# A gated spectral and MLP block with its gradients: the gate as row sums on VectorE, the first products by pairs of token blocks, the last tile in halves

## The chip, the core and the metric

The kernel runs on one core of a Trainium2 chip. The metric is the device time of one execution in microseconds (us). The time before is the median of nine runs.

## The reference

Inputs are bf16: x and grad_out (2048 tokens of 1024), a spectral filter w (2048 x 513, real and imaginary part), w1 (1024 x 3584), b1, w2 (3584 x 1024), b2 and a gate vector of 1024. What is computed, cut to its core:

```
g = sigmoid((x * gate_w).sum(-1, keepdims=True))       # one number for each token
a = irfft2(rfft2(x) * (w_r + 1j * w_i))                # spectral branch
h = relu(x @ w1 + b1) ** 2                             # the MLP branch
b = h @ w2 + b2
out = g * a + (1 - g) * b
```

The kernel returns the output and its gradients for x, w_r, w_i, w1, b1, w2, b2 and gate_w: nine results. Both branches take the same x (the input A_x); the input B_x is not used.

## The kernel before, in words

Tokens are held in 16 tiles of 128; tile i takes every 16th row. The work runs in stages on TensorE (PE), and the spectral transforms run beside them as a side generator, a few steps at a time.

**First stage, `mlp_in`.** For each pair of hidden blocks (`fp`, 14 pairs, 256 hidden columns each) and each of four blocks of 512 tokens (`s`), two kinds of unit run. `forth` makes a 128x512 block of the hidden layer: eight products from `w1` and the turned tokens `xT` (L725), Relu and Square on ScalarE (ACT; L726, L727). `back_` makes the same block of its gradient: eight products from turned `w2T` and the turned, gated gradient `dbT` (L733), and one VectorE instruction (DVE; L737) that multiplies it by Relu's output. Both write to two PSUM banks in turn. For the first two pairs, the order is four `forth` units and four `back_` units for each block of tokens: 32 units. While they run, the tiles they need are made: `turn_tile` transposes a 128x1024 tile by eight products with an identity (L640) into a PSUM tile of which there are two, and a copy on ACT or DVE takes it to `xT` or `dbT` (L641). The loop at the end of the program writes this order out by hand, between calls of `next(units)`.

**The gate.** `gate(i0)` makes the gate of four tiles on PE: 32 products with one column (L655), two sigmoids on ACT (L659, L660), and four DVE multiplications that scale the gradient rows `dbn` by 1 - g (L662). `turn_grad` needs the scaled rows.

**Loads at the start.** `ld` issues on the SP queue, `st` on GpSimd's. SP issues the tokens `xsrc` (4 x 256 KB), `w1g` (512 KB), the gradients `dbn` (4 x 256 KB), the second `w1g`, and `w2T` by transposing DMAs. GpSimd's queue loads the constants `kf`, `flip`, `sel` and `cf`; ACT's queue the identity and the vectors b1 and gate_w, which `vectors` turns into columns. `warm` puts blank products on PE.

**Side work.** `first_stage_of_x` takes one tile through `folds` (six DVE instructions and some ACT copies), `row_stage` (L277, eight products on PE, copy on ACT) and `first_columns` (L310, copies on ACT, two DVE additions, stores).

**Middle.** The weight gradients follow (L987), then `mlp_out`: out = h @ w2 for blocks of 256 tokens and the gradient of x, each block by a scheme of seven products of half size (`p1` to `p7`; `chain`, L1339), with sums of operands on DVE (L1335) and partial results copied by ACT (`kept`, L1349) and added by DVE (`add`, L1360). The inverse transforms run beside the first part of it; `folded` copies `re` on ACT (L553) and forms `rf` on DVE (L558, L559).

**The end.** The last blocks of the gradient of x: `prepare_x` (L1300, L1301 on ACT, L1302 and L1307 on DVE) prepares the two tiles of a block, `close_x` (L1311, L1312) adds and stores a tile. For the last block, `gacc` is transposed and reduced on DVE (L1583, L1585), and a small product `prow` (L1591) makes the gradient of gate_w.

The compiler orders the instructions of an engine by the program's order and by readiness in its own account. Ties written by hand override this: `in_turn`, `pe`, `dve` and `act` tie an instruction behind the last one that was so marked, without a semaphore. In `mlp_out`, every instruction marked `act` stands behind the one marked before it:

```python
        def act(ins):
            after(ins, turn["ACT"], mybir.DependencyClass.NoSync)
            turn["ACT"] = ins
```

Of the kernel before, what the change touches and what calls it, by code (L numbers as in the profile page):

```python
# [10 lines left out]
P = 128  # L11
# [129 lines left out]
def kernel(  # L141
# [67 lines left out]
    gwcol = cols("gwcol", [DC], BF16)  # L209
# [31 lines left out]
    turn = {"PE": None, "DVE": None, "ACT": None}  # L241
# [288 lines left out]
    def fft_out():  # L530
# [15 lines left out]
        def folded(n):  # L546
# [5 lines left out]
            for im in range(2):  # L552
                in_turn(nc.scalar.copy(  # L553
                    out=evens[n][:, im].rearrange("p g (h i) -> p g h i", h=2),
                    in_=rv[:, im, :, 0::2, :].rearrange("p h g i -> p g h i"),
                ), "ACT")
# [74 lines left out]
    def source(i, view, earlier=None, tag="src"):  # L631
        src = f1.tile([P, D], BF16, name=tag, tag=tag, bufs=4)
        after(ld(out=src[:], in_=view[i]), earlier)
        return src

    def turn_tile(dst, i, src, copy):

        pt = tps.tile([P, DC, P], BF16, name="pt", tag="tr", bufs=2)
        for b in range(DC):
            nc.tensor.transpose(pt[:, b, :], src[:, b * P : (b + 1) * P], identb[:])  # L640
        copy(out=dst[:, :, of_tile(i)], in_=pt[:])  # L641

    def vectors(vrow):
        vps = tps.tile([P, FC + DC], BF16, name="vps", tag="tr", bufs=2)
        nc.tensor.transpose(vps[:], vrow[:], identb[: FC + DC, : FC + DC])
        nc.vector.tensor_copy(out=b1col[:], in_=vps[:, 0:FC])
        nc.vector.tensor_copy(out=gwcol[:], in_=vps[:, FC : FC + DC])

    def gate(i0):

        c_ = slice(i0, i0 + 4)
        pg = tps.tile([P, 4], FP32, name="pg", tag="tr", bufs=2)
        for i in range(i0, i0 + 4):
            for dc in range(DC):
                mm(  # L655
                    pg[:, i - i0 : i - i0 + 1], lhsT=xT[:, dc, of_tile(i)], rhs=gwcol[:, dc : dc + 1],
                    start=(dc == 0), stop=(dc == DC - 1), skip_group_check=True,
                )
        nc.scalar.activation(omg[:, c_], pg[:], ACT.Sigmoid, scale=-1.0)  # L659
        nc.scalar.activation(gcol[:, c_], pg[:], ACT.Sigmoid)  # L660
        for i in range(i0, i0 + 4):
            nc.vector.tensor_scalar(out=dbn[:, i, :], in0=dbn[:, i, :], scalar1=omg[:, i : i + 1], scalar2=None, op0=ALU.mult)  # L662
# [37 lines left out]
    def mlp_in():  # L700
# [41 lines left out]
        def load_w2(fg, earlier=None):  # L742

            w2T[fg] = wb.tile([P, DC, FGW], BF16, name="w2T", tag="w2T", bufs=2)
            for h in (0, FGW // 2):
                f0 = fg * FGW + h
                after(turned(w2T[fg][:, :, h : h + FGW // 2], B_w2[f0 : f0 + FGW // 2, :]), earlier)
# [5 lines left out]
        def load_w1(fp):  # L753
            w1[fp] = wb.tile([P, DC, PW], BF16, name="w1g", tag="w1g", bufs=2)
            ld(out=w1[fp][:], in_=w1v[:, :, fp * PW : (fp + 1) * PW])

        def forth(fp, s, c):
            rT = rTs[fp, s, c] = wb.tile([P, SW], BF16, name="rT", tag="rT", bufs=6)
# [24 lines left out]
        load_w1(0)  # L783
        yield
        load_w1(1)
        load_w2(0)
        yield
        for s in range(4):
            for what in (forth, back_):
                for fp in range(2):  # L790
                    for c in range(2):
                        what(fp, s, c)
                        yield
            if s == 2:
                load_w1(2)
# [13 lines left out]
    def mlp_grads():  # L809
# [151 lines left out]
        class Turned(Block):  # L961
# [8 lines left out]
            def kept(self, name, bufs=1):  # L970
                t_ = sb.tile([P, H], FP32, name=name, tag=name, bufs=bufs)
                turn["ACT"] = nc.scalar.copy(out=t_[:], in_=self.X[:])
# [234 lines left out]
    def mlp_out():  # L1207
# [106 lines left out]
        class Block:  # L1314
# [32 lines left out]
            def kept(self, name, bufs, where=None):  # L1347
                t_ = wb.tile([P, H], FP32, name=name, tag=name, bufs=bufs)[:] if where is None else where
                act(nc.scalar.copy(out=t_, in_=self.X[:]))  # L1349
                return t_  # L1350
# [33 lines left out]
            def p7(self):  # L1384
                self.chain(self.X, self.S[3], self.B["T3"], False)
                self.u3 = self.kept("u3", 1)
                self.add(1, R, self.V, self.u3)
# [40 lines left out]
        for t, hf in steps:  # L1428
# [4 lines left out]
            act(nc.scalar.copy(out=fresh(t)[:, (L, R)[hf]], in_=acc[:]))  # L1433
            if hf:
# [25 lines left out]
        for k in range(N0, NB):  # L1460
# [41 lines left out]
            if last:  # L1502
                right(T1, qs[1], qs[0])
            if a is not None:
                put(2 * k - 2)
            prepare(2 * k + 1), prepare(2 * k)
            if not last:
# [57 lines left out]
        for k in range(2, NB):  # L1565
# [9 lines left out]
            if k > 2:  # L1575
                a.p3()
            b.p5()
# [8 lines left out]
            b.p7()  # L1586
            a = b
        a.done = lambda t: close_x(t, ld)
        a.p4()
# [4 lines left out]
        a.p3()  # L1594
# [33 lines left out]
    def turn_x(i):  # L1628
        turn_tile(xT, i, rows.pop(i), nc.vector.tensor_copy if i in (1, 3) else nc.scalar.copy)
# [17 lines left out]
    units = mlp_in()  # L1647
    rows_of_x(0)
    vrow = f1.tile([FC + DC, P], BF16, name="vrow", tag="vrow")
    nc.scalar.dma_start(out=vrow[0:FC, :], in_=B_b1.rearrange("(fc p) -> fc p", p=P))  # L1650
    nc.scalar.dma_start(out=vrow[FC : FC + DC, :], in_=gate_w.rearrange("(fc p) -> fc p", p=P))
    next(units)
    rows_of_grad(0)
    st(out=kf[:], in_=cten["kf"].ap())
    st(out=flip[:], in_=cten["flip"].ap())
    st(out=sel[:], in_=cten["sel"].ap())
    for i in range(4):
        turn_x(i)
        warm((0, 2, 3, 0)[i])
    vectors(vrow)  # L1660
    warm(2)
    next(units)
    rows_of_x(1)
    st(out=cf[:], in_=cten["cf"].ap())
    stage = None
    for k in range(NT // 4):
        i = 4 * k
        if k + 1 < NT // 4:
            rows_of_grad(k + 1)
        next(units)  # L1670
        if k == 0:
            gate(0)
        else:
            turn_grad(i), turn_grad(i + 1)
        next(units)
        turn_grad(i + 2) if k else (turn_grad(i), turn_grad(i + 1))
        next(units)
        turn_grad(i + 3) if k else (turn_grad(i + 2), turn_grad(i + 3))
        next(units)
        if stage:  # L1680
            next(stage)
        next(units)
        if k + 1 < NT // 4:
# [113 lines left out]
```

## Time and profile before

| what | value |
|---|---|
| median of 9 runs | 1216.16 us (1215.03 to 1220.24) |
| profiled execution | 1218.06 us, its span 1216.3 us |
| PE busy | 1189.4 us, 98% of the span |
| DVE, ACT, GpSimd busy | 827.5, 621.3, 362.0 us |
| DMA | 234.44 MB, mean 193 GB/s |
| first product of `mlp_in` (L725) | starts at 12.06 us |
| last product (L1339) | ends at 1210.50 us |

The span runs from the first instruction to the last; the profiled execution's own time has 1.8 us outside it. Rows give the start in us, the duration or the busy time in us, engine, line and operation, with output and inputs by the program's names; a bracket holds the idle time of the engine ahead of it and what ended it. The clock is the share of full speed that TensorE was granted. Names of buffers can hide what is in them: `even` is also the scaled gate vector, `w2R` also `gacc` and its sums, `odd` and `even` the blocks of the hidden layer.

### The profile page before, as it was taken

What the parts mean: (1) busy time and instruction counts of PE and PEld (TensorE: products, weight loads), DVE (VectorE), ACT (ScalarE), POOL (GpSimd) and SP (SyncE); (2) the same over time, 40 slices, a digit from 0 to 9 for tenths busy, and PEclk for the clock granted to TensorE, in tenths of its full rate; (3) what the DMA queues carried; (4) which work ended last, traced back from release to release, by engine and by line L of the source; (5) the groups of instructions that cost most, each with busy time, mean ns of one, the idle gap of its engine ahead of it and who ended that gap; (6) DMA issues with size and microseconds to landing.
All of it is one profiled execution on the core that took longest, in us unless ns stands there. A gap on an engine that the chain in (4) does not pass through costs nothing. (4 is left out here: it accounts for less than half of the span.)

```text
span 1216.3 us, 20077 instructions
## 1 busy us (share of the span) xinstructions
PE 1189.4 (98%) x7229; PEld 653.8 (54%) x7328; DVE 827.5 (68%) x1808; ACT 621.3 (51%) x1128; POOL 362.0 (30%) x587
## 2 busy tenths in 40 slices
PE   8999999999999999999999999999999999999997
PEld 4555545544444444444447888898444444444443
DVE  2656456686788986888779557665389756966464
ACT  4557767746777774444444255554454432332322
POOL 0124424413445541333434444444231000000000
PEclk9999999999999999999999999999999999999999
DMA  9657667585758598899998799955975699965540
GB/s 265 226 156 181 179 151 218 158 161 184 213 171 212 182 228 169 184 224 204 239 201 169 164 241 234 207 170 170 272 222 173 188 214 227 242 198 175 158 149 35
DMA packets 332382, 234.44 MB, mean 193 GB/s; under 512 B 197772, under 2 KB 291114, under 8 KB 332282
## 3 DMA queue, kind: packets, MB, share of 16 engines
q1 hardware_dynamic: 301856, 142.50, 51.3%
q0 software_dynamic: 30224, 90.61, 23.9%
q8 instruction: 57, 0.93, 0.3%
q14 instruction: 43, 0.35, 0.1%
q10 hardware_dynamic: 202, 0.04, 0.0%
HBM read 107.24 MB, written 81.81 MB: 155 GB/s over the span
## 5 line engine op out<-in xcount | busy, mean ns | idle before, releaser
L725 PE MATMUL ph<-xT,w1g 128*128 128x512 bf16 x866 | 216.1, 381 | 3.2 <-DMA w1g<-in_B_w_dram 1.2
L733 PE MATMUL pd<-dbT,w2T 128*128 128x512 bf16 x874 | 210.0, 379 | 1.0
L733 PEld LDWEIGHTS <-w2T 128*128 128x128 bf16 x896 | 87.1, 98 | 101.8
L737 DVE SCALAR_TENSOR_TENSOR dhT<-pd,rT 128x512 bf16<-128x512 f32 x112 | 76.9, 687 | 88.5 <-PE pd L733 75.4
L725 PEld LDWEIGHTS <-w1g 128*128 128x128 bf16 x896 | 85.6, 98 | 94.2 <-issue 1.6
L726 ACT ACTIVATE rT<-ph,b1col 128x512 bf16<-128x512 f32 x112 | 77.3, 690 | 69.8 <-PE ph L725 67.2
L987 PEld LDWEIGHTS <-res 128*128 128x128 bf16 (+1 forms) x896 | 86.7, 98 | 12.3 <-issue 2.0
L1339 PEld LDWEIGHTS <-dS 128*128 128x128 f16 x574 | 55.9, 98 | 66.4
L226 POOL DMA_DIRECT2D z_scr<-u x96 | 58.8, 618 | 105.3 <-ACT u L294 50.9
L226 POOL DMA_DIRECT2D r<-y_scr x96 | 58.5, 614 | 104.3 <-issue 44.2
L419 ACT CAST x<-px 64x512 f16<-64x512 f32 x128 | 74.2, 579 | 18.0 <-PE px L416 16.9
L727 ACT ACTIVATE h2T<-rT 128x512 bf16<-128x512 bf16 x112 | 70.5, 630 | 2.1
L987 PEld LDWEIGHTS <-X 128*128 128x128 f16 x672 | 64.8, 98 | 8.0
L1339 PEld LDWEIGHTS <-odd 128*128 128x128 bf16 (+1 forms) x392 | 38.3, 98 | 47.7 <-issue 2.1
L1339 PEld LDWEIGHTS <-even 128*128 128x128 bf16 (+1 forms) x392 | 38.1, 98 | 44.6
L913 PEld LDWEIGHTS <-S 128*128 128x128 f16 x336 | 32.9, 98 | 39.7 <-DVE S L887 0.3
L456 POOL DMA_DIRECT2D y_scr<-pc x64 | 36.4, 569 | 52.6 <-DVE pc L453 43.5
L779 POOL DMA_DIRECT2D h2T_scr<-h2T x28 | 20.7, 740 | 98.2 <-ACT h2T L727 98.0
L1360 DVE TENSOR_TENSOR cu<-pV,u 128x512 f16<-128x512 f32 x28 | 19.3, 690 | 44.0 <-PE pV L1339 38.3
L568 ACT CAST rt<-pki 128x1024 f16<-128x1024 f32 x32 | 32.4, 1013 | 29.2 <-PE pki L566 29.2
L1312 POOL DMA_DIRECT2D out_dram<-gxo x14 | 7.6, 542 | 131.8 <-DVE gxo L1311 131.8
L426 DVE TENSOR_TENSOR tt<-x,w 128x1028 f16<-128x1028 f16 (+1 forms) x32 | 22.2, 694 | 33.8 <-ACT x L420 20.8
(265 smaller groups left out, 2472.8 us busy)
## 6 DMA issues: line engine op xcount, KB each, us to landing
h2T_scr<-h2T POOLq DMA_DIRECT2D x28, 512.0 KB, 4.3
dhT_scr<-dhT POOLq DMA_DIRECT2D x28, 512.0 KB, 5.2
z<-z_scr SPq DMA_DIRECT2D x64, 128.0 KB, 3.1
y_scr<-pc POOLq DMA_DIRECT2D x64, 128.0 KB, 3.4
ax_scr<-yo POOLq DMA_DIRECT2D x32, 256.0 KB, 4.1
w1g<-in_B_w_dram SPq DMA_DIRECT2D x14, 512.0 KB, 4.6
out_dram<-whi POOLq DMA_DIRECT2D x28, 256.0 KB, 4.4
out_dram<-wlo POOLq DMA_DIRECT2D x28, 256.0 KB, 4.5
```

Source lines behind the costliest of these rows:

```text
L226: issue(out=a, in_=b) if stored else issue(out=b, in_=a)
L419: nc.scalar.copy(out=x[lanes[n], c, :, 0:HW], in_=px[lanes[c], n])
L456: st(out=y_scr[:][c, :, :, h].rearrange("r x t l -> (r x) t l"), in_=pc[:, n])
L568: nc.scalar.copy(out=rt[n][:], in_=pk[:])
L725: mm(ph[:], lhsT=w1g[:, dc, fc % 2 * P : (fc % 2 + 1) * P], rhs=xT[:, dc, ss], start=(dc == 0), stop=(dc == DC - 1))
L726: nc.scalar.activation(rT[:], ph[:], ACT.Relu, bias=b1col[:, fc : fc + 1])
L727: nc.scalar.activation(h2T, rT[:], ACT.Square)
L733: mm(pd[:], lhsT=w_[:, ec, fc % FGC * P : (fc % FGC + 1) * P], rhs=dbT[:, ec, ss], start=(ec == 0), stop=(ec == DC - 1),)
L737: return STT(out=dhT, in0=pd[:], scalar=2.0, in1=rT[:], op0=ALU.mult, op1=ALU.mult, accum_out=gb1part[:, fc, sb : sb + 1],)
L913: self.mm = mm(acc[:], lhsT=lhs[:, t, c_], rhs=rhs[:, t, :], start=start and t == 0, stop=t == KH - 1, skip_group_check=True,)
L987: ins = mm(acc[:, j * FH : (j + 1) * FH], lhsT=lhs[:, t, c_], rhs=rhs[:, t, :], start=start and first_ is None, stop=t == KH - 1, skip_gro ...
L1339: pe(mm(acc[:], lhsT=lhs[:, c, :], rhs=rhs[:, c, :], start=start and c == 0, stop=c == KH - 1, skip_group_check=True,))
```

## The change

- The gate: `gate_w` is spread over the partitions by two products of one row of ones (`everywhere`, into `gwb`); `weigh` multiplies a token tile by it and sums each row in one DVE instruction, as each tile is turned. `gate` reads the sums; its 32 products go. The b1 column is turned alone, earlier.
- Loads: the first `w1g` goes out on ACT's queue, the second ahead of the gradients. Eight `xsrc` buffers take the place of four, so that the next four tiles are requested at once, ahead of `w2T`. The constants on GpSimd's queue wait for the first gate.
- The 32 units: two blocks of tokens are taken together, eight `forth` units and then eight `back_` units. One tile is turned behind a unit; a step of the side work comes behind every second unit from the 13th on (ten steps instead of eleven).
- Ties: `re` is tied to a chain of its own, `copy`, which holds only copies out of PSUM, in place of `ACT`.
- `mlp_out`: for the last hidden block, the sum T1 is put behind `put` and `prepare`. For the last block of the gradient, the u3 product and its copy stand ahead of p5; the addition that uses the copy stays where it was.
- The last tile: its left half is added and stored early; u2 is added to the prepared rows in advance; the last product runs in two halves of 256 columns, each added and stored by itself.

```diff
@@ turns
-    turn = {"PE": None, "DVE": None, "ACT": None}
+    turn = {"PE": None, "DVE": None, "ACT": None, "copy": None}
@@ folded: the copies of re
-                ), "ACT")
+                ), "copy")
@@ the gate
+    def everywhere(grow, ones):
+        pb = fps.tile([P, D], FP32, name="pgw", tag="ps2", bufs=2)
+        for h in range(2):
+            later["gate_row"] = mm(pb[:, h * H : (h + 1) * H], lhsT=ones, rhs=grow[:, h * H : (h + 1) * H], start=True, stop=True)
+        gwb = f1.tile([P, D], BF16, name="gwb", tag="gwb")
+        nc.scalar.copy(out=gwb[:], in_=pb[:])
+        return gwb
+
+    def weigh(i, src):
+        unused = f1.tile([P, 2, H], FDT, name="uv", tag="uv", bufs=2)
+        weighed = nc.vector.tensor_tensor_reduce(
+            out=unused[:].rearrange("p a b -> p (a b)"), in0=src[:], in1=gwb[:], scale=1.0, scalar=0.0,
+            op0=ALU.mult, op1=ALU.add, accum_out=gsum[:, i : i + 1],
+        )
+        after(weighed, later.get("b1"), mybir.DependencyClass.NoSync)
...
-        pg = tps.tile([P, 4], FP32, name="pg", tag="tr", bufs=2)
-        for i in range(i0, i0 + 4):
-            for dc in range(DC):
-                mm(
-                    pg[:, i - i0 : i - i0 + 1], lhsT=xT[:, dc, of_tile(i)], rhs=gwcol[:, dc : dc + 1],
...
-        nc.scalar.activation(omg[:, c_], pg[:], ACT.Sigmoid, scale=-1.0)
-        nc.scalar.activation(gcol[:, c_], pg[:], ACT.Sigmoid)
+        nc.scalar.activation(omg[:, c_], gsum[:, c_], ACT.Sigmoid, scale=-1.0)
+        nc.scalar.activation(gcol[:, c_], gsum[:, c_], ACT.Sigmoid)
@@ mlp_in
-        load_w1(0)
+        load_w1(0, nc.scalar.dma_start)
         yield
         load_w1(1)
-        load_w2(0)
         yield
-        for s in range(4):
+        load_w2(0, later["row"], mybir.DependencyClass.NoSync)
+        yield
+        for pair in range(2):
             for what in (forth, back_):
-                for fp in range(2):
-                    for c in range(2):
-                        what(fp, s, c)
-                        yield
-            if s == 2:
-                load_w1(2)
+                for s in (2 * pair, 2 * pair + 1):
+                    for fp in range(2):
+                        for c in range(2):
+                            what(fp, s, c)
+                            yield
+                if pair and what is forth:
+                    load_w1(2)
+            if not pair:
                 load_w2(1, later["last"])
@@ mlp_out, last hidden block
             for _ in made:
                 pass
-            if last:
-                right(T1, qs[1], qs[0])
             if a is not None:
                 put(2 * k - 2)
             prepare(2 * k + 1), prepare(2 * k)
+            if last:
+                right(T1, qs[1], qs[0])
@@ mlp_out, last block of the gradient
             if k > 2:
                 a.p3()
+            if last:
+                b.u3_kept()
             b.p5()
             b.sums(4)
             prepare_x(2 * k), prepare_x(2 * k + 1)
...
-            b.p7()
+            if last:
+                b.add(1, R, b.V, b.u3)
+            else:
+                b.p7()
             a = b
         a.done = lambda t: close_x(t, ld)
+        t_ = 2 * (NB - 1)
+        c_, v_, o_ = cu.pop(t_), v.pop(t_), row("gxo", BF16, tag="ot")
+        dve(V(out=o_[:, L], in0=c_[:, L], in1=v_[:, L], op=ALU.add))
+        ld(out=o1_perm[t_][:, L], in_=o_[:, L])
+        dve(V(out=c_[:, R], in0=v_[:, R], in1=a.u2, op=ALU.add))
         a.p4()
...
-        a.p3()
+        for j in range(2):
+            c2 = slice(j * H // 2, (j + 1) * H // 2)
+            d2 = slice(H + j * H // 2, H + (j + 1) * H // 2)
+            a.chain(a.V[:, c2], a.S[4], a.B["22"][:, :, c2], False)
+            dve(V(out=o_[:, d2], in0=a.V[:, c2], in1=c_[:, d2], op=ALU.add))
+            ld(out=o1_perm[t_][:, d2], in_=o_[:, d2])
@@ the start
     units = mlp_in()
+    grow = f1.tile([1, D], BF16, name="grow", tag="grow")
+    nc.scalar.dma_start(out=grow[:], in_=gate_w.rearrange("(o d) -> o d", o=1))
+    next(units)
...
     for i in range(4):
         turn_x(i)
-        warm((0, 2, 3, 0)[i])
-    vectors(vrow)
-    warm(2)
+        warm((0, 2, 2, 0)[i])
+        if i == 1:
+            vectors(vrow)
+    gate(0)
+    rows_of_x(1)
     next(units)
-    rows_of_x(1)
...
+    rows_of_grad(1)
+    for t_, n in ((kf, "kf"), (flip, "flip"), (sel, "sel"), (cf, "cf")):
+        after(st(out=t_[:], in_=cten[n].ap()), later["scaled"])
     stage = None
-    for k in range(NT // 4):
...
+    for u in range(32):
         next(units)
...
+        if u < 4:
+            turn_x(u + 4)
+        elif u < 12:
+            turn_grad(u - 4)
+        elif u < 20:
+            turn_x(u - 4)
+        elif u < 28:
+            turn_grad(u - 12)
+        if u in (4, 16, 20):
+            gate(4 if u == 4 else u - 8)
+        if u == 4:
+            rows_of_x(2)
+            rows_of_grad(2)
+            rows_of_grad(3)
+        if u == 11:
+            for n in range(3):
+                xs[n] = source(n, x_perm)
             stage = first_stage_of_x()
+        if u == 15:
+            rows_of_x(3)
+        if u > 11 and u % 2:
+            next(stage)
```

## The prediction

> **What bounds the kernel now.** I read the page's sections 1 and 2 first: TensorE (PE) is busy 98% of 1216.3 us. So time is won only where PE waits, runs below full clock, or does work that can be dropped. Next I asked for the busy time in chosen stretches, to see where the start loses:
>
> ```profile
> 5.20:8.60 3.40, 2.22 (x22) 1.12 (x19) 0.69 (x1) 1.58 (x2) 0.00 (x0) 1.00 0.90 307
> 8.60:12.06 3.46, 1.28 (x11) 0.69 (x12) 0.85 (x3) 0.44 (x1) 0.00 (x0) 1.00 1.08 364
> 12.06:15.46 3.40, 3.18 (x8) 1.20 (x10) 0.00 (x0) 0.00 (x0) 0.00 (x0) 0.50 1.56 150
> ```
>
> The columns are length, busy PE, PE weight loads, VectorE (DVE), ScalarE (ACT) and GpSimd, then granted clock, DMA share and GB/s. The first real product (L725) starts at 12.06, and the first eight run at clock 0.50. A stretch with 2.22 of 3.40 us busy was followed by full clock, one with 1.28 of 3.46 by half clock. From 12.06 to 75 us PE is busy 61.75 of 62.94 us: 1.2 us idle in the whole phase of the first 32 units. The timeline gives what stands around the first products:
>
> ```profile
> 9.54 0.62 PE L640 MATMUL pt<-identb,xsrc 128*128 128x128 bf16 x8 [1.12 <-DMA xsrc<-in_A_x_dram]
> 12.06 1.03 PE L725 MATMUL ph<-xT,w1g 128*128 128x512 bf16 x2 [1.25 <-DMA w1g<-in_B_w_dram]
> 49.67 0.94 PE L655 MATMUL pg<-gwcol,xT 128*128 128x1 bf16 x32
> ```
>
> Token tile 3 lands at 9.5 us and w1 at 12.06, so w1 ends the wait. A gate takes 32 small products. For the end I read the chain of waits, in order of time (start, length, what):
>
> ```profile
> 1200.31 3.04 PE pX L1339 x14
> ...
> 1203.36 0.59 ACT u L1349
> ...
> 1204.00 3.18 PE pX L1339 x14
> ...
> 1210.53 0.70 DVE cu L1360
> ...
> 1211.25 0.69 DVE gxo L1311
> ```
>
> PE waits for the copy of u3 (1203.36), and after its last product at 1210.50 two additions and a 256 KB store remain. The waits from 850 us on name the rest of what the change touches:
>
> ```profile
> PE pX L1339 <- ACT u L1349: 1.5, 2, 0.9
> PE pki L566 <- ACT re L553: 1.5, 1, 1.5
> ```
>
> **Start: first product.** Three moves act on 12.06 us: w1 goes ahead on ACT's queue, the constants kf, flip, sel and cf (0.38 MB) leave the first microseconds, and b1 and the gate row are split. With w1 landed, tile 3 remains. Unchanged it lands at 9.54, then eight transposes (0.62) and an ACT copy (1.01): 11.2. The other end: the DMA view shows 1.70 MB moved by 8 us; w1 and four tiles are 1.6 MB, and at 0.28 MB/us the constants were 1.3 us of it. So 6.7 + 1.6 = 8.3. I take 10.0 because the shared engines still carry w1's second pair and the gradients: gain 2.1, ends 0.9 and 3.8. A rule speaks against the second queue here. The Trainium skill ("DMA: Bandwidth & Descriptors", Issuing engines are not separate DMA queues) says that transfers issued from several engines interleave on the same DMA engines and save only issue time. By it alone the gain would be the 0.9 us of the late end.
>
> **Start: clock.** Eight products at 0.425 us instead of 0.216 lose 1.7 us. In the new order, 8.6 to 12.06 holds tile 3's transposes and 2 us of products, as much as the stretch that kept full clock. Gain 1.7, ends 0 and 1.7.
>
> **Gate.** On PE, 128 products with N = 1 go. From 49.67 to the next row at 50.48 one gate of 32 takes 0.81 us; four are 3.2 us, all on PE's path. On DVE come 16 row sums. The nearest row, L1269 (128x1024, multiply and sum), is 1.22 us and 0.08 for its accumulator: 20.9 us. DVE is busy 32.0 of the 62.9 us, so 53 of 63 afterwards. That fits on average; where it does not is in the next part. The two products that spread the gate row fall into the wait for tiles and cost nothing; without that wait they cost 0.9 (two at 0.43).
>
> **Start: order by pairs.** A unit is eight products (1.73 us) and one tile's transposes (0.44, from 57.96 to 60.13 less 1.73). Before, the last tile of a block was turned a unit or more ahead of its use. Now tile 7 is turned behind unit 3 and read by unit 4, and so at seven joints: PE must wait for the copy out of PSUM. Behind a forward unit ACT first does Relu (0.69) and Square (0.63), then copies in 1.01; with 0.2 of latency, about 2.0 us after the transposes. That is at units 3 and 19. At 15 ACT is free: 1.2. On DVE a copy takes 0.69: 0.9 at units 7 and 23, and 1.2 at 11 and 27, where L737 goes first. The sum is 9.4. Filling: the next tile's transposes (0.44 at six joints) and the side transform's columns (0.53 at three) leave 5.2. The compiled order has such filling already (row products L277 stand inside a unit at 36.38). It can go further, and the old 1.2 us of waits belonged to the old order, which leaves -1.2 as the lower end and 9.4 as the upper. Tile 4 is also requested just ahead of use (about 12.5 against 11.7): 0.8. I take 2.9 net, below the middle. DVE and ACT are hidden behind PE elsewhere; where four row sums meet four L737 and two folds (units 12 to 15: L737 with its accumulator 0.77 and a row sum 1.3, four times, and folds of 2.3, four rows of 0.42 and two of 0.29, twice: 12.9 against PE's 10) that cover is gone, and up to 2.9 more could show, but the next four units have no L737 and take it back.
>
> **Queues.** SP: w1(0) leaves it, w1(1) stands ahead of the gradients, and the next four tiles' rows ahead of w2's transposes. Those were issued from 9.5 to 19.1 and are wanted only behind eight units now, near 29 us. POOL: the four constants wait for the first gate; behind them stands nothing until the first h2T store at 39.8. Neither costs.
>
> **Middle.** At 1036 PE waits 0.87 for u, which stands in ACT's order behind `na`, which waits for L1278, which waits behind the 3.88 us subtraction L1399. The change puts T1 behind those: -0.9, ends 0 and -0.9. At 899.7 PE waits 1.5 for `re`; freed of ACT's order, it next meets `rf` on DVE (L558, at 899.72 for 0.28). I take -0.3, ends 0 and -1.5.
>
> **End.** Gains: PE's 0.64 wait for u3 goes if the last p4 finds X free. After the last product one 128x256 addition (0.4, half of 0.69 and some overhead) stands instead of 0.69 + 0.72: -1.0. The last store is 64 KB instead of 256: at 362 GB/s, -0.5. But the diff also moves ACT's work. `act` ties every ACT instruction to the one before it, and u3_kept now stands ahead of prepare_x:
>
> ```profile
> 1194.78 1.06 ACT L1300 ACTIVATE gy<-gx 128x1024 f16<-128x1024 f16 x1
> ...
> 1199.66 0.68 DVE L1302 TENSOR_TENSOR g<-gy,even 128x1024 f16<-128x1024 f16 x1
> ...
> 1204.76 1.22 DVE L1585 TENSOR_REDUCE w2R<-w2R 128x32 f32<-128x1024 f32 x1
> 1205.90 0.68 DVE L1360 TENSOR_TENSOR cu<-pV,u 128x512 f16<-128x512 f32 x1
> ```
>
> The u3 chain takes p5's slot and ends at 1200.31, so its copy ends at 1200.9 and gy starts there, not at 1194.78. Then gy and scaled (1.06 + 1.14) let DVE's g start at 1203.0, 3.3 later; the second g is 3.4 later, and with it the sum, the transpose, the reduction and the addition that reads V: it ends at 1209.98 instead of 1206.58. Behind it in PE's order stand prow and both halves: p3 starts at 1210.0 instead of 1207.36, +2.65. So the 0.64 is not won, and +2.65 - 1.0 - 0.5 = +1.1. PE is then nearly idle from 1206.5 to 1210.0, like the stretch at 8.60 that was followed by half clock: the 3.06 us of halves could lose up to 1.7; I take 1.0. End: +2.1, ends -2.1 (all goes as meant, 0.64 included) and +2.8. The skill's clock rule ("TensorE: Matmul & The Clock Gate", What's actually happening) says an idle window of about 3.4 us halves the clock; by it the loss would be nearer 1.7, as at 12.06.
>
> **Sum.** -2.1 - 1.7 - 3.2 + 2.9 = -4.1 at the start, -1.2 in the middle, +2.1 at the end: -3.2. The profiled execution took 1218.06 (span 1216.3 and 1.8 outside it), 1.9 above the median; taken from the median 1216.16 this gives 1213.0.
>
> **Rivals.** First: the joints fill (net 0.5, not 2.9): 1210.6. For it speaks how little PE idles now; against, that unit 4 needs tile 7. 0.2. Second: the end also works, because ACT runs by readiness: -4.2 more, 1206.4. Against it stand four ACT rows in exactly the order of the code. 0.12. Third: the joints cost their 5.2: 1215.3, no change that can be told. 0.15. Fourth, slower: the copies out of PSUM become the bound, ACT in forward units (Relu, Square, copy: 2.3 us against PE's 2.17), so that the joints cost all 9.4: 1219.5. It decides from 6.1 us on, where the sum is zero. 0.13. That w1 on another queue moves nothing is within the forecast's 0.9.
>
> **Numbers.** The forecast has 0.40, and its own spread is 1211.5 to 1215. A measurement of this kernel tells about 0.2%, 2.4 us, from no change: the border is 1213.7. Faster is 0.6 of the forecast's 0.40 and the first two rivals, 0.56; I put 0.54, the rest to the third. Same 0.31, slower 0.15. The range from 1208.0 to 1217.5 leaves out most of the second rival and of the fourth.
>
> **What would show it.** Right: L725 starts near 10 at clock 1.00; no L655; waits of PE for xT and dbT copies (L641) at every fourth unit, some 3 us in all; at 1036 no wait for u; gy of the last block behind the u3 copy, and PE idle some 3 us ahead of the last two halves. Wrong: gy ahead of u3's copy and no such idle time (then about 1208), or joints over 6 us (then no gain).

## The result, and the profile after

| what | before | after |
|---|---|---|
| median | 1215.83 us (55 executions) | 1225.69 us (18 executions, 1223.34 to 1237.48) |
| ratio | | 1.0087, 95% interval 1.0067 to 1.0106 |
| profiled execution | 1218.06 us | 1237.48 us |

The change is slower by 0.9%. The prediction was 1213.0, its range ended at 1217.5. After's profiled execution is the longest of the 18, so it is read for where time goes, and sizes are taken from the experiments too. Line numbers moved: L725 is now L734, L733 is L742, L641 is L642, L1339 is L1355.

**The start.** Same stretches and columns as before (length, busy PE, weight loads, DVE, ACT, GpSimd, clock, DMA share, GB/s):

```profile
8.60:12.06 3.46, 0.00 (x0) 0.00 (x0) 0.52 (x2) 0.00 (x0) 0.00 (x0) 0.93 1.09 356
12.06:15.46 3.40, 2.15 (x18) 1.93 (x19) 2.50 (x5) 2.11 (x4) 0.00 (x0) 0.50 0.85 302
15.46:18.90 3.44, 3.22 (x13) 1.38 (x13) 3.20 (x7) 0.14 (x2) 0.07 (x1) 0.57 1.16 192
```

PE does nothing for 3.46 us, then stays at half clock through two stretches instead of one. The timeline names the wait:

```profile
12.15 0.20 PE L646 MATMUL vps<-identb,vrow 28*128 28x28 bf16 x1 [5.17 <-DMA vrow<-in_B_b_dram]
12.28 1.89 PE L641 MATMUL pt<-identb,xsrc 128*128 128x128 bf16 x16
...
13.35 1.93 ACT L642 COPY xT<-pt 128x1024 bf16<-128x1024 bf16 x2 [6.28 <-PE pt L641]
...
15.33 1.44 PE L734 MATMUL ph<-xT,w1g 128*128 128x512 bf16 x3 [1.16 <-ACT xT L642]
```

The b1 rows are 7 KB, but they were requested on ACT's queue behind the 512 KB of w1, and landed with them. PE waits for them in order, the transposes of token tiles 2 and 3 stand behind, then two ACT copies in a row. The first product starts at 15.33.

**The first stage and the weight gradients.** Again by stretches:

```profile
20.00:100.00 80.00, 75.25 (x561) 43.47 (x570) 52.09 (x131) 45.17 (x89) 14.33 (x23) 1.00 0.64 195
255.00:300.00 45.00, 43.49 (x226) 19.92 (x228) 36.53 (x67) 18.68 (x31) 9.84 (x12) 1.00 0.67 175
690.00:800.00 110.00, 105.50 (x1046) 93.81 (x1043) 58.10 (x160) 51.60 (x96) 47.37 (x77) 1.00 1.16 187
```

From 20 to 100 PE is idle for 4.75 us (1.32 before): the joints, where PE reads a tile that has only just been turned. From 255 to 300 it loses 1.5 where it lost 0.2. From 690 to 800 the DMA share is 1.16 (0.99 before) for fewer bytes, and PE loses 4.5 (1.7 before). The longest standstill comes right after. PE waits for `rf`, and `rf` stands in DVE's order behind an instruction that waits for a transposing load (`even`):

```profile
806.85 0.29 PE L566 MATMUL pki<-ki,rf 128*128 128x128 f16 x1 [8.36 <-DVE rf L558]
```

```profile
803.09 1.23 DVE L1051 TENSOR_TENSOR G<-even,G 128x2048 f16<-128x2048 bf16 x1 [2.92 <-DMA even<-dhT_scr]
...
806.51 0.29 DVE L558 TENSOR_TENSOR rf<-r 128x256 f16<-128x256 f16 x1
```

**The end.**

```profile
1217.01 0.59 ACT L1365 COPY u<-pX 128x512 f32<-128x512 f32 x1 [5.46 <-PE pX L1355]
1217.49 1.06 ACT L1316 ACTIVATE gy<-gx 128x1024 f16<-128x1024 f16 x1
...
1226.08 0.25 PE L1622 MATMUL prow<-sel,w2R 128*32 128x32 f32 x2 [3.06 <-DVE w2R L1608]
...
1226.67 3.10 PE L1355 MATMUL pV<-w2L,dS 128*128 128x256 bf16 x14 [0.35 <-DVE cu L1377]
...
1230.28 1.69 PE L1355 MATMUL pV<-w2L,dS 128*128 128x256 bf16 x14 [0.52 <-DVE gxo L1629]
```

gy stands behind the copy of u3, PE waits 3.06 us for the reduction, and the first half runs at half clock (3.10 against 1.69).

### The profile page after: what moved, and what is told of

It is laid out like the page before. It is cut to its first block, busy times and chain, and to the rows that moved or that the text cites. A ratio compares the mean times of both kernels' runs of the same rounds, so it can differ in the third digit from the quotient of the medians.

```text
span 1235.7 us, 19910 instructions
## 1 busy us (share of the span) xinstructions
PE 1191.7 (96%) x7116; PEld 653.5 (53%) x7213; DVE 844.5 (68%) x1841; ACT 624.8 (51%) x1130; POOL 364.8 (30%) x587
## 5 line engine op out<-in xcount | busy, mean ns | idle before, releaser
L734 PE MATMUL ph<-xT,w1g 128*128 128x512 bf16 x867 | 215.3, 381 | 5.7 <-ACT xT L642 3.9
L742 PE MATMUL pd<-dbT,w2T 128*128 128x512 bf16 x874 | 209.4, 379 | 3.5 <-DVE dbT L642 1.4
L742 PEld LDWEIGHTS <-w2T 128*128 128x128 bf16 x896 | 87.1, 98 | 106.1 <-issue 3.7
L734 PEld LDWEIGHTS <-w1g 128*128 128x128 bf16 x896 | 85.9, 98 | 96.9 <-issue 4.9
L746 DVE SCALAR_TENSOR_TENSOR dhT<-pd,rT 128x512 bf16<-128x512 f32 x108 | 74.3, 688 | 78.6 <-PE pd L742 70.2
L735 ACT ACTIVATE rT<-ph,b1col 128x512 bf16<-128x512 f32 x108 | 74.6, 691 | 48.6 <-PE ph L734 45.6
L1355 PEld LDWEIGHTS <-dS 128*128 128x128 f16 x588 | 57.9, 99 | 68.1 <-issue 1.7
L1355 PEld LDWEIGHTS <-odd 128*128 128x128 bf16 (+1 forms) x392 | 38.2, 98 | 45.1
L1355 PEld LDWEIGHTS <-even 128*128 128x128 bf16 (+1 forms) x392 | 38.1, 98 | 44.6
L1355 PE MATMUL pX<-wT,dS 128*128 128x512 f16 x196 | 44.8, 379 | 0.5 <-DVE dS L1351 0.5
L394 POOL COPY w<-wn 128x512 bf16<-128x512 bf16 x32 | 23.5, 736 | 68.9 <-DVE tt L427 60.1
```

Source lines behind the costliest of these rows:

```text
L734: mm(ph[:], lhsT=w1g[:, dc, fc % 2 * P : (fc % 2 + 1) * P], rhs=xT[:, dc, ss], start=(dc == 0), stop=(dc == DC - 1))
L735: nc.scalar.activation(rT[:], ph[:], ACT.Relu, bias=b1col[:, fc : fc + 1])
L742: mm(pd[:], lhsT=w_[:, ec, fc % FGC * P : (fc % FGC + 1) * P], rhs=dbT[:, ec, ss], start=(ec == 0), stop=(ec == DC - 1),)
L746: return STT(out=dhT, in0=pd[:], scalar=2.0, in1=rT[:], op0=ALU.mult, op1=ALU.mult, accum_out=gb1part[:, fc, sb : sb + 1],)
L1355: pe(mm(acc[:], lhsT=lhs[:, c, :], rhs=rhs[:, c, :], start=start and c == 0, stop=c == KH - 1, skip_group_check=True,))
```

## The experiments

All times are medians, each beside executions of before on the same chip (1215.3 to 1215.7). Diffs are against the kernel named.

### What before usually does

Three of the kernels below have exactly the start of before. Their profiles are not like the one that the prediction read. This is halves_alone, first its timeline, then its stretches:

```profile
10.71 1.90 PE L725 MATMUL ph<-xT,w1g 128*128 128x512 bf16 x8 [1.23 <-DMA w1g<-in_B_w_dram]
```

```profile
8.60:12.06 3.46, 2.23 (x15) 0.94 (x12) 0.85 (x3) 0.06 (x1) 0.00 (x0) 1.00 1.07 365
12.06:15.46 3.40, 3.40 (x52) 2.22 (x51) 1.67 (x4) 1.73 (x5) 0.00 (x0) 1.00 1.24 230
...
20.00:100.00 80.00, 79.13 (x669) 45.65 (x668) 42.15 (x121) 49.94 (x99) 16.63 (x26) 1.00 0.67 210
255.00:300.00 45.00, 45.00 (x239) 20.78 (x238) 34.11 (x74) 23.00 (x40) 11.86 (x18) 1.00 0.67 175
690.00:800.00 110.00, 108.34 (x1091) 97.04 (x1089) 69.06 (x197) 56.63 (x107) 49.37 (x80) 1.00 0.98 218
```

The first product starts at 10.71 (10.18 in end_alone, 10.09 in before_ten), at full clock; in halves_alone and end_alone the rest of the first stage runs 3.0 and 3.6 us ahead of its place in the profile of before. The profiled execution of before, at 1218.06, was one with a late w1 and half clock behind it. Of the 97 executions of before that were timed beside the experiments, 80 have a mean clock of 0.999 or 1.000; the profiled one had 0.997.

### The start

**after_again**: the changed kernel without an edit.

> The changed kernel itself, as the base for the others. In the profiled execution of it the first product starts at 15.33 us, PE is some 3.1 us idle ahead of the prow product at the end, and PE stands still for some 9 us between 797 and 807 us, where the inverse transform waits for its DMAs. Theory (three separate losses: start 3.4, end about 3, side work 1.4): about 1223.5 us, and without the standstill near 800 us. Rival (the standstill near 800 us is part of the change and the main loss): it shows here again with 8 us or more.

1236.08 us (1227.4 to 1242.1), not the 1223.5 that was expected, and above the 1225.69 of the result. The profile has the same waits at the start and at the end, with the first product at 13.8. When it starts depends on the execution, the wait for b1's rows does not. The standstill near 800 us is not in this profile: the longest wait of PE between 690 and 850 is 2.0 us.

**b1_first**: b1's rows requested ahead of w1.

```diff
+    vrow = f1.tile([FC, P], BF16, name="vrow", tag="vrow")
+    nc.scalar.dma_start(out=vrow[:], in_=B_b1.rearrange("(fc p) -> fc p", p=P))
     next(units)
...
     rows_of_x(0)
-    vrow = f1.tile([FC, P], BF16, name="vrow", tag="vrow")
-    nc.scalar.dma_start(out=vrow[:], in_=B_b1.rearrange("(fc p) -> fc p", p=P))
```

> One edit: the row b1 is issued on ACT's queue ahead of w1, not behind it. PE's order is the same. Theory (PE waits in order for b1's 28 short rows, which arrive behind 512 KB of w1; the transposes of tiles 2 and 3 stand behind b1's): the first product moves from 15.3 to about 12.5 us, the whole by -2.5 to -3, and up to -1.7 more if the clock then stays full. Rival (the bytes bound the start: w1's last packets come at 11.5 us on the second queue too, tile 3 no sooner): the first product at 12 us at best, never near 10. Second rival (two ACT copies in a row set it): b1 early brings under 1 us.

1229.43 us, first product at 12.00, half clock in one stretch instead of two; the first stage runs 0.2 to 0.5 behind the profile of before instead of 3.4. The start is mended by 3 us, but the time scatters from 1221 to 1240, and PE stands still around 785.

**one_queue**: w1 back on SP's queue, ahead of the tokens.

```diff
-        load_w1(0, nc.scalar.dma_start)
+        load_w1(0)
```

> The changed kernel with the first w1 back on SP's queue (ahead of the tokens in SP's order), b1 still on ACT's. Theory: b1's rows, behind nothing on ACT's queue, land by 5 us; the late tiles 2 and 3 no longer stand behind them, and the first product starts at 11 to 12.2 instead of 13.8 to 15.3: 2 to 3 us faster than the changed kernel (near 1221). Rival: the shared engines carry the same bytes, so tile 3 comes last instead and nothing is won: 1223.5.

1228.08 us, first product at 12.06. At 94 us it is 3.2 ahead of the changed kernel, but in its profile PE is idle for 5.9 us between 700 and 800. With b1's rows out of the way the first product starts at 12.0 on either queue (12.00 in b1_first), and waits there for an ACT copy of a turned tile (1.10 and 1.57 us), not for w1. So the second queue gains nothing, and with b1 behind w1 it costs. The Trainium skill ("DMA: Bandwidth & Descriptors", Issuing engines are not separate DMA queues) says that another issuing engine saves only issue time; no gain beyond that shows in these runs. They add that the order within the queue counts for what stands behind a large transfer.

**turn_ahead**: each tile turned ahead of its unit instead of behind it.

```diff
     for u in range(32):
-        next(units)
         if u < 4:
             turn_x(u + 4)
...
             turn_grad(u - 12)
+        next(units)
```

> One edit: in the loop of 32 units a tile is turned ahead of the unit of its number, not behind it, so that the fourth tile of a block stands one unit ahead of its use. Theory (seven joints at which PE waits for a copy out of PSUM, 3.4 us in all): PE's idle time between the first product and the 32nd unit falls from about 4.7 to about 1.5 us: -2 to -3.4, less what tile 4, turned ahead of the first unit, waits for its arrival (up to 1). Rival (the idle time is DVE's overload by the row sums): it stays above 3 us.

1222.35 us. PE busy from 20 to 90, turn_ahead and then the changed kernel:

```profile
20.00:90.00 70.00, 68.83 (x518) 39.94 (x527) 46.64 (x117) 39.39 (x78) 11.13 (x17) 1.00 0.65 204
```

```profile
20.00:90.00 70.00, 65.36 (x493) 37.88 (x500) 45.56 (x112) 39.80 (x77) 11.04 (x18) 1.00 0.65 198
```

One unit of lead takes away 3.5 us of waits: the joints are as the prediction described them, and are avoidable. (The time can't be set against this alone: the first product of this profile starts at 12.38, not at 15.33.)

**gate_alone**: before with the row sums in place of the gate's products, each ahead of its tile's turn; nothing else.

```diff
     def turn_x(i):
+        src = rows.pop(i)
+        weigh(i, src)
-        turn_tile(xT, i, rows.pop(i), nc.vector.tensor_copy if i in (1, 3) else nc.scalar.copy)
+        turn_tile(xT, i, src, nc.vector.tensor_copy if i in (1, 3) else nc.scalar.copy)
```

> The kernel before with one edit: the gate as row sums on DVE (16 of 1.2 us), its 128 PE products gone, two products for the spread row ahead of the tiles. Theory: 3.2 us less on PE's path and all of it stays, about 1212.6. Rival: the row sums stand ahead of the L737 products and of the copies of turned tiles on DVE, so that PE waits for DVE in the first 75 us what it saved; then 1215 to 1217, and the row sums are why the joints of the changed kernel cost 3.4 us.

1222.43 us: 7 us slower, with 3.2 us of PE work less. In DVE's order, copies out of PSUM stand behind row sums: the first behind four, the second behind three, the first of which had waited for its tokens until 20.38. PE waits 3.88 and 3.16 us for these copies:

```profile
10.79 1.22 DVE L658 CUSTOM_DVE_ANT_0 uv<-xsrc,gwb 128x1024 f16<-128x1024 bf16 x1
11.94 0.08 DVE L658 DVE_READ_ACCUMULATOR2_ANT gsum<- 128x1 f32 x1
11.94 0.69 DVE L641 COPY xT<-pt 128x1024 bf16<-128x1024 bf16 x1
...
23.95 1.28 DVE L641 COPY dbT<-pt 128x1024 bf16<-128x1024 bf16 x2
```

```profile
12.68 6.23 PE L732 MATMUL ph<-xT,w1g 128*128 128x512 bf16 x16 [3.88 <-DVE xT L641]
...
24.69 1.76 PE L640 MATMUL pt<-identb,dbn 128*128 128x128 bf16 x16 [3.16 <-DVE dbT L641]
```

**gate_later**: gate_alone with each row sum tied behind the copy of its tile, the first four behind all four first copies.

```diff
+        after(weighed, later["copy"], mybir.DependencyClass.NoSync)
...
+        if i > 3:
+            weigh(i, src)
+        elif i == 3:
+            for n in range(4):
+                weigh(n, first[n])
```

> The kernel before with the gate as row sums, as in the run gate_alone, but each row sum put behind the copy of its tile on DVE, the first four behind the copies of all four first tiles. Theory: gate_alone lost because DVE works in order and copies of turned tiles stood behind up to four row sums (3.88 us at the first product, 3.16 at 24.7, and half clock after both); with the copies ahead the first wait goes and the second shrinks below 1: 1212 to 1216. Rival: DVE's load itself (20.9 us more in the first 75) is what PE waits for, wherever it stands: 1220 or more.

1214.21 us, ratio 0.9984 (0.9969 to 0.9998): first product at 10.66, full clock, no wait of PE over 1.5 us in the first stage. The same 16 row sums cost 7 us or gain 1.3 by their place in DVE's order. Of the 3.2 us of PE work, 1.3 became time.

### The end

**p7_back**: the changed kernel with u3 and its copy back in their place.

```diff
-            if last:
-                b.u3_kept()
             b.p5()
...
-            if last:
-                b.add(1, R, b.V, b.u3)
-            else:
-                b.p7()
+            b.p7()
```

> One edit: the u3 product and its copy of the last block stand behind the preparation again, as before; the halves stay. Theory (ACT's tie holds the preparation of the last two tiles behind the u3 copy, and the reduction, prow and the halves wait for it): gy starts some 6 us earlier against the p6 product, no 3 us wait ahead of prow, the half clock there gone; -2.7 to -4. Rival (the halves themselves cost it, by the wait of the second for the addition of the first): the wait ahead of prow goes, but the time between the last p4 and the end shrinks by under 1 us.

1230.04 us, scattered from 1221.6 to 1243, so the time tells little. The profile, of the longest of the nine executions, tells more about the end: no wait for the reduction, and 1.3 us of idle PE from 1200 on instead of 4.0.

**end_alone**: before with the whole new end (u3 ahead of p5, u2 added in advance, halves); **halves_alone**: the same without the move of u3.

> The kernel before with the edits of the end alone: u3 and its copy ahead of p5 in the last block, last tile in halves, u2 added in advance. Theory: the end loses 2.8 us as in the changed kernel, because gy, scaled, g, the reduction and prow stand behind the copy of u3: about 1218.6, a wait of PE for the reduction of about 3 us, and half clock in the two halves. Rival: the loss at the end of the changed kernel came from its other edits (DMA late in that execution); then 1214, no wait of 3 us.

> The kernel before with the last tile in halves and u2 added in advance, but u3 where it was. Theory: no wait for the reduction, full clock, one 128x256 addition and a 64 KB store behind the last product instead of two additions and 256 KB: 1.0 + 0.5 less, and up to 0.5 lost where the second half waits for the first half's addition: about 1214.5 (1213.8 to 1215.2). Rival: the halves bring nothing because the wait between them and the store's fixed time eat it: 1216.

1220.1 and 1216.13 us. At 1185 us both still run at the pace of before (3.5 and 2.8 ahead of its profile); their spans end 0.6 and 2.8 ahead. So the move of u3 costs 2.9 us, and the halves bring nothing. (The medians differ by 4.0, but both scatter.) The end of end_alone:

```profile
1205.88 0.25 PE L1604 MATMUL prow<-sel,w2R 128*32 128x32 f32 x2 [3.06 <-DVE w2R L1590]
...
1206.48 3.15 PE L1339 MATMUL pV<-w2L,dS 128*128 128x256 bf16 x14 [0.35 <-DVE cu L1360]
```

In halves_alone the two halves run at full clock, but the second waits 0.52 for the addition of the first, so from the first product of p3 to the end of the last addition are 4.4 us instead of 4.65; and from there to the end of the span are 4.6 instead of 4.3, in spite of the smaller store.

The time from that last addition to the end of the span differs from profile to profile. The time from another store does not: GpSimd's store of prow's row, the gradient of gate_w. Here it is in before, halves_alone, end_alone and the changed kernel:

```profile
1208.91 0.54 POOL L1593 DMA_DIRECT2D out_dram<-w2R  x1 [9.33 <-DVE w2R L1592]
```

```profile
1206.11 0.54 POOL L1598 DMA_DIRECT2D out_dram<-w2R  x1 [9.34 <-DVE w2R L1597]
```

```profile
1208.34 0.54 POOL L1606 DMA_DIRECT2D out_dram<-w2R  x1 [12.30 <-DVE w2R L1605]
```

```profile
1228.54 0.53 POOL L1624 DMA_DIRECT2D out_dram<-w2R  x1 [12.29 <-DMA out_dram<-gxo]
```

Their spans end at 1216.3, 1213.5, 1215.7 and 1235.7: 7.4, 7.4, 7.4 and 7.2 us after that row starts. In all 17 profiles it is 7.2 to 7.5 us, while the last addition ends 2.7 to 4.6 us ahead of the end. halves_alone is 2.8 ahead of before and issues this store 2.8 earlier: the halves do not touch it. end_alone is 3.5 ahead and issues it only 0.6 earlier: that is the 2.9. No run moves this store by itself, so that the end hangs on it is read from the profiles, not tried.

### The eleventh step

**eleven**: the changed kernel with eleven steps of the side work among the 32 units, as before, instead of ten.

```diff
-        if u > 11 and u % 2:
+        if u > 10 and u % 2:
             next(stage)
```

> The changed kernel with eleven steps of the side work among the 32 units, as before, instead of ten. Theory: with ten steps the side work is one step behind all through the first stage, and PE waits behind bunches of side instructions on DVE from 255 to 300 us (1.4 to 2.0 us more than before). With eleven steps those waits fall back to about 0.2 us, the start stays as it was, so the time is about 1.7 us under the changed kernel's (near 1221.7 in undisturbed executions). Rival: the waits at 255 to 300 us come from the late start of the first stage (everything is 3.4 us later against the same loads); then they stay and the time does not move. Second question: if the late landings of DMA between 700 and 830 us come from the side work being a step behind, the DMA share of 700 to 750 us falls from 1.18 to the 1.05 of before, and few executions lie above 1229.

1223.29 us (1221.6 to 1230.8). PE is busy 45.00 of 45 us from 255 to 300, the DMA share of 700 to 800 is 1.00, there is no standstill. The lag behind the profile of before stays at 3.5 us from 100 to 1027, and is 2.7 at 1067: the moved T1 gains 0.8 (0.9 forecast). Against the 1225.69 of the result the eleventh step gives back 2.4 us.

**before_ten**: the kernel before, one step less, nothing else.

```diff
             stage = first_stage_of_x()
-        next(stage)
+        if k:
+            next(stage)
         next(units)
         next(stage)
```

> The kernel before with one edit: ten steps of the side work among the 32 units instead of eleven. Theory: the missing step alone costs 1.3 to 2.2 us from 255 to 300 us (PE busy near 43.5 of 45 there instead of 45.0), lifts the DMA share of 700 to 800 us from 0.96 to 1.1 or more, and makes executions of 5 to 20 us more common: median 1217.5 to 1224. Rival: the step only moves work that hides behind PE anywhere, and the two signs in the changed kernel come from its later start: 1215.5, PE busy 45.0.

1221.7 us, ratio 1.0037 (1.0013 to 1.006): 6.4 us slower by the medians, 4.5 by the ratio, because six executions lie at 1216.9 to 1220.0 and six at 1223.4 to 1224.7. The profiled one is of the longer six. One step brings all the signs, from a start that is as in before:

```profile
255.00:300.00 45.00, 43.66 (x230) 19.98 (x228) 35.44 (x73) 22.78 (x38) 12.01 (x17) 1.00 0.56 152
690.00:800.00 110.00, 102.26 (x1003) 90.38 (x1002) 63.33 (x173) 50.99 (x95) 45.98 (x74) 0.97 1.17 195
```

```profile
796.31 0.29 PE L566 MATMUL pki<-ki,rf 128*128 128x128 f16 x1 [6.50 <-DVE rf L558]
```

The DMA queues from 690 to 800 us (packets, MB, share of 16 engines), halves_alone with eleven steps, then before_ten:

```profile
q1 hardware_dynamic: 35591, 11.32, 56.3%
q0 software_dynamic: 4404, 12.52, 41.0%
```

```profile
q1 hardware_dynamic: 30959, 10.45, 70.9%
q0 software_dynamic: 3807, 10.78, 45.3%
```

With fewer packets done, the share is higher. On q1, which carries the transposing loads and w2, a packet takes 0.563 x 16 x 110 us / 35591 = 27.8 ns with eleven steps and 40.3 with ten. The same sum for every kernel here gives 28 to 31 ns in the nine profiles with eleven steps and 32 to 44 in the eight with ten.

**mended2_ten**: the run mended2 (below) with ten steps.

> The run mended2 with ten steps instead of eleven, nothing else. Theory: as for before_ten, 1.3 to 2.2 us from 255 to 300 us and a fuller DMA at 700 to 800: 1215.5 to 1222 against 1213.6. Rival: 1213.6, no difference.

1217.03 us (1212.3 to 1230.0) against 1213.64 (1212.4 to 1220.3). The forecast 1.3 to 2.2 us at 255 to 300 were 0.4 (PE busy 44.57), yet the DMA share of 690 to 800 is 1.18 against 0.97, with about the same number of packets (39730 and 39482). The profiled execution, 1212.79, is one of the shortest: there PE is busy 108.06 of the 110 us, and loses nothing in spite of that share. So with ten steps the DMA is fuller in each profile, and whether PE then stands still differs from one execution to the next.

**one_queue_eleven**: one_queue with eleven steps.

> The changed kernel with two edits: the first w1 back on SP's queue, and eleven steps. Against the run eleven (1223.3) this shows the second queue alone. Theory: the first product starts near 12.0 instead of 14.1, and the lost 2 to 3.5 us show in the time because the DMA between 700 and 800 us is not overfull: 1219.5 to 1221.5. Rival: the queue is worth nothing in the time: 1223.3.

1219.87 us (1219.5 to 1221.3), first product at 12.31. Against eleven the second queue (with b1 behind it) is 3.4 us, about what the two profiles differ by at the start: the first product comes 1.8 earlier, and the first eight take 1.89 us instead of 3.57. So here the gain at the start shows in the time, as it did not in one_queue.

### Put together

**mended**: b1_first, turn_ahead, p7_back and eleven in one.

> The changed kernel with four repairs: b1's rows requested ahead of w1, each tile turned ahead of its unit instead of behind it, eleven steps of the side work, u3 and its copy back in their place. Theory (the losses are these four, each by itself, against a usual execution of before that starts its first product near 10.4 at full clock): the gate's 3.2 us stay won, T1 wins 0.8, the halves 0.4, the first product costs 1 to 1.6 because tile 3 waits for b1col and a copy on ACT, and half clock may cost 1.7: net -1 to -3.5, 1212 to 1214.5. Rival: the losses share a cause (DVE has too much to do at the start), and move elsewhere when one is undone: 1216 to 1219.

1218.1 us. The middle is as forecast, the 0.4 us of the halves did not come, and the start is not as forecast: tile 3's transposes wait for b1's column on DVE, the first product starts at 12.0, tile 4, now turned ahead of unit 0, has not landed (1.76 us at 14.4), and PE runs at half clock from 13.0 for 6.8 us. The four losses were not the whole start.

**mended2**: besides, b1's column first, tiles 1 and 3 copied on DVE ahead of all row sums, the second four token tiles requested ahead of the gradients, tile 4 turned behind unit 0. Against mended:

```diff
-        after(weighed, later.get("b1"), mybir.DependencyClass.NoSync)
+        after(weighed, later["copy"], mybir.DependencyClass.NoSync)
...
+    rows_of_x(1)
     rows_of_grad(0)
-    gwb = everywhere(grow[:], ones[:])
+    vectors(vrow)
+    first = [rows.pop(n) for n in range(4)]
     for i in range(4):
-        turn_x(i)
+        if i == 2:
+            gwb = everywhere(grow[:], ones[:])
+        turn_tile(xT, i, first[i], nc.vector.tensor_copy if i % 2 else nc.scalar.copy)
         warm((0, 2, 2, 0)[i])
-        if i == 1:
-            vectors(vrow)
+    for i in range(4):
+        weigh(i, first[i])
     gate(0)
-    rows_of_x(1)
     next(units)
...
         if u < 4:
-            turn_x(u + 4)
+            if u:
+                turn_x(u + 4)
...
         next(units)
+        if not u:
+            turn_x(4)
```

> As the run mended, with the start reordered besides: the b1 column first on PE and DVE, copies of tiles 1 and 3 on DVE ahead of all row sums, the second four token tiles requested ahead of the gradients, tile 4 turned behind unit 0. Theory: w1 lands near 9, tile 3 by 7 and nothing waits behind a row sum, so the first product starts at 9.0 to 9.6, full clock, 1.2 us ahead of a usual start of before: 1210 to 1212. Rival: the first products then wait for the second four tiles or for DVE at the first gradient tiles, and it is no faster than mended.

1213.64 us, ratio 0.9977 (0.9956 to 0.9999): the lowest median here, though gate_later's 1214.21 can't be told from it. Its start:

```profile
10.53 1.90 PE L734 MATMUL ph<-xT,w1g 128*128 128x512 bf16 x8 [0.16 <-DMA w1g<-in_B_w_dram]
12.26 0.78 PE L641 MATMUL pt<-identb,xsrc 128*128 128x128 bf16 x11
12.88 1.89 PE L734 MATMUL ph<-xT,w1g 128*128 128x512 bf16 x8
```

Full clock, no waits of PE between units 0 and 3. The forecast 9.0 to 9.6 for the first product was not met: w1 did not land earlier than in a usual start of before.

## Why the prediction was wrong, step by step

- **First product (-2.1) and clock (-1.7): failed, and for two reasons.** Most of the gain was not there: 12.06 at half clock belonged to one execution, the usual one has 10.1 to 10.7 at full clock. The prediction noted that its profile lay 1.9 us above the median, and then took gains measured on that execution from the median. And the move itself lost: b1's wait and the two copies put the first product at 15.33, 5.0 us behind a usual start, and half clock until 18.4 costs about 1.5 more (3.1 us of products at half speed). This is the step of the prediction that failed first: it costed b1's rows at nothing and did not ask what stands behind them in PE's order.
- **Gate (-3.2): the size on PE held, the cover did not.** "53 of 63" of DVE was an average. gate_alone shows that the order decides, from -1.3 to +7. The changed kernel copies tile 3 on ACT, which costs it two ACT copies in a row.
- **Joints (+2.9 net): right in mechanism, somewhat small.** PE is idle 4.75 us from 20 to 100, against 0.87 in a usual execution of before: +3.9. turn_ahead takes it back.
- **Ten steps instead of eleven: not priced at all.** The description of the change names it, and the prediction costs nothing between 100 and 850 us. before_ten alone is 4.5 to 6.4 us slower: in its profile PE loses 1.3 us at 255 to 300, where row additions of the gradient's sum come in bunches on DVE ahead of the instruction that PE waits for, and 7.7 from 690 to 800 (1.7 in halves_alone), where the DMA is fuller. In the changed kernel the eleventh step alone gave back 2.4.
- **Middle (-1.2).** T1's 0.8 came. The wait for `re` turned into one for `rf`, as said (1.81 at 903.5 in eleven): nothing gained of the 0.3.
- **End (+2.1): the delay was right, the rest of the sum was not, and that +2.9 was measured is partly luck.** The copy of u3 holds back gy, the reduction and prow as forecast, and p3 starts 2.7 later (2.65 forecast; 1206.48 in end_alone against 1207.29 less its lead of 3.5). But the prediction took the kernel to end with p3, its additions and its store. It ends 7.2 to 7.5 us after the store of prow's row, and that store goes out 3.0 us later. By this reading the other terms are there and count for nothing: the additions give 0.3 instead of 1.0 because of the wait between the halves, and half clock costs 1.45 instead of 1.0. The Trainium skill's clock rule ("TensorE: Matmul & The Clock Gate", What's actually happening) put the half-clock term nearer 1.7; the run lies between it and the estimate.

The sum for the changed kernel, against a usual execution of before: +5.0 +1.5 -3.2 +3.9 = 7.2 at the start (the lag measured at 100 us is 3.4 + 3.3 = 6.7), +1.5 at 255 to 300, -0.8 for T1, +2.9 at the end: about +10, and before has 1215.3 to 1215.8. The median was 9.9 longer. That the two agree so well is partly chance: the sum holds nothing for the fuller DMA, to which the profiled execution lost another 11 us between 750 and 940, and some executions start earlier than 15.33.

Of the rivals, none had the right place. The slower one (the copies become the bound) reached 1219.5 by the joints alone; the joints were not the cause.

What stays open: why a packet on the queue of the transposing loads takes 40 ns instead of 28 once the side work runs one step later. The requests are the same in kind and size; their place against each other differs. Nor is it known why end_alone and halves_alone scatter (five of twelve executions each are more than 4 us above the fastest) when their first 1185 us are those of before.

## What to carry to other kernels

Hold the profiled execution's own time against the median before taking a wait from it: a gain read from a slow start is partly no gain, and two profiles of an unchanged start would have shown it. When work moves to another engine, ask for every copy and every small load what now stands ahead of it: here the place of 16 row sums, not their 21 us of load, made the difference between -1.3 and +7. Count the steps of interleaved side work before and after a loop is rewritten: one step less, with no wait of its own, cost the kernel before 4.5 to 6.4 us. And look for what the end of the span follows before shortening the last product: here it was a store of 2 KB on another engine.

## What was not expected of the hardware

- The same kind of packets, in the same stage, took 28 to 31 ns each in the nine profiles with eleven steps of the side work and 32 to 44 in the eight with ten (0.737 x 16 x 110 / 29355 in the changed kernel), and PE then stood still for up to 8 us in some executions and not at all in others.
- The column of the granted clock can be silent. In eleven it reads 1.00 in all three stretches from 8.60 to 18.90, but the first eight products took 3.57 us, against 1.90 at full clock in halves_alone: the first clock record of that trace stands at 20.07 us. The durations of the products show the half clock, the column does not.

```profile
14.14 3.57 PE L734 MATMUL ph<-xT,w1g 128*128 128x512 bf16 x8 [1.16 <-ACT xT L642]
```

- A 7 KB load behind a 512 KB load on the same queue kept PE waiting until 12.15 us in the changed kernel; requested ahead of it, it was there when PE came to it at 8.7.
- The span ended 7.2 to 7.5 us after GpSimd began to issue a 2 KB store, whatever came after that store on the other engines.
